# Attention values for two query blocks in one step, ten probability tiles, and another spread of the filling matmuls

## The chip, the cores and the metric

The kernel runs on one core of a Trainium2 chip. The metric is the device time of one execution in microseconds (us), the median of three runs. The core has five engines with instruction queues of their own: TensorE (PE in the profile, its weight loads PEld), VectorE (DVE), ScalarE (ACT), GpSimd (POOL) and SyncE (SP), which here issues the DMA transfers.

## The reference

`x` has 2048 tokens of 512 numbers. It is normalized; from the normalized `xn` comes an attention with 32 heads of 16 numbers over a sliding window of 256 keys, and a two-layer network whose output gates it:

```python
xn = layernorm(x)
q, k, v = split(xn @ wqkv)                      # 32 heads of 16
scores = q k^T / 4, kept where 0 <= i - j < 256
o = softmax(scores) @ v
s = o @ wo
g = silu(gelu(layernorm(xn) @ w1 + b1) @ w2 + b2)   # 512 -> 1792 -> 512
out = x + s * g
```

All inputs and outputs are 32-bit floats.

## The kernel before, in words

**Stages.** A short first stage normalizes `x`, transposes it (`xnT`) and makes the first queries, keys and values. Then comes the attention (72 to 448 us of the profiled execution), and after it the network and the gating.

**Slots.** The attention is one loop `for t in range(-16, end + 1)` whose passes are called slots here. The 32 heads are eight groups `n` of four heads; the 2048 tokens are sixteen blocks of 128. Slot `t` from 0 to 127 works on group `t // 16` and block `t % 16`. In program order a slot issues:

1. `prob_block(.., 1)`: two matmuls put the scores of one pair of heads (keys in the partitions, 384 queries) into `stb`, ScalarE takes their exponential into a tile `pt` (`ACT pt<-stb` in the profile), GpSimd clears the two corners outside the window (`affine_select`).
2. `max_block` for the block `LEAD` = 12 slots ahead: eight matmuls into `xy` and `zo`, then VectorE masks (`COPY_PREDICATED xy<-upper,zo`) and takes the maxima (`TENSOR_REDUCE mt<-xy`). Slots from 116 on have none.
3. `fill_in(t, 0)`: fills, matmuls of other work (`fb<-...`), and then the steps that are planned for this slot with `at`.
4. `prob_block(.., 0)`, the other pair of heads, into the same `stb`.
5. `fill_in(t, 1)`: more fills.
6. `pv_step` for block `t - 1`: values times probabilities of the three key blocks that the window touches, four heads side by side in column groups of 32 (17 weights columns each: 16 values and a column of ones for the sum). ScalarE copies the result out of PSUM (`oraw<-zo`).
7. Steps that are planned with `behind`, mostly DMAs.

Items 1 to 3 are called the first part of a slot here, items 4 to 7 the second part. `stb` exists once, so the scores of one part wait until ScalarE has read those of the part before. A matmul instruction of 32-bit floats (`pv_step`) is two passes in the profile, so the twelve of a step are recorded as x24; most other matmuls are of the type F32R and are recorded once.

**Dependencies by tile.** `otb`, in which `pv_step` accumulates, is a part of the PSUM tile `zo`; `max_block` uses another part of it. The built program makes the first matmul of `pv_step` wait for VectorE's masking of the same slot, and the next `max_block` matmul into `zo` wait for ScalarE's copy of `otb`.

**Fills.** `tandem(t0, t1, one, two)` lays two jobs over slots `t0` to `t1`: projections of queries and keys (`pair_qk`), of values (`pair_v`), or of the network's hidden layer (`pair_h`). Two matmuls with 64 rows each run side by side and make one unit; a tandem has two phases of 12 units (512 columns) or 24 (256 columns). Before, most units lie in the first part: typically three units of 512 columns there and one, two or three in the second part. At `t1` ScalarE and VectorE copy the two results out.

**Queries and keys.** `pair_qk(n, c).finish` plans, for a later slot `free`, a copy of the projection on ScalarE into a tile `sh` (`hi`, the rounded upper part), behind it four DMAs out of `sh` into the slot tile `qk` (`qk<-sh`), and in a slot given by `quiet` a subtraction on GpSimd that reads `sh` (`pjr<-pjr,sh`). `sh` has two buffers. The copies of jobs `c` and `c + 1` are two to four slots apart.

Of the kernel before, what the change touches and what calls it, by code (L numbers as in the profile page):

```python
# [9 lines left out]
F32 = mybir.dt.float32  # L10
F32R = mybir.dt.float32r
# [38 lines left out]
def mixer_kernel(ctx, tc, x, wqk, wv, wo, w1, b1, w2, b2, out):  # L50


    nc = SimpleNamespace(**{name: Ordered(tc, name) for name in ("tensor", "vector", "scalar", "gpsimd", "sync")})
# [6 lines left out]
    attn = ExitStack()  # L60
    psum = attn.enter_context(tc.tile_pool(name="psum", bufs=1, space=PSUM))
    vp = attn.enter_context(tc.tile_pool(name="vp", bufs=1))
    pp = attn.enter_context(tc.tile_pool(name="pp", bufs=8))
    sgp = attn.enter_context(tc.tile_pool(name="sgp", bufs=1))

    PASSES = ((0, 0), (0, 1), (1, 0))
# [78 lines left out]
    slots = []  # L145
# [16 lines left out]

    xy = psum.tile([P, 2, 512], F32, name="xy")
    zo = psum.tile([P, 2, 512], F32, name="zo")
    otb = zo[:, 1, 256:384]
    psf = attn.enter_context(tc.tile_pool(name="psf", bufs=1, space=PSUM))
    fb = [psf.tile([P, 512], F32, name=f"fb{i}") for i in range(2)]
    early = ExitStack()
# [99 lines left out]
    def job_qk(n, c):  # L268

        box = []  # L270
        ops = [(kt, a, b) for kt in range(KT) for a, b in PASSES]
        if not n and c < 2:
            ops.sort(key=lambda o: o[2])
        sl = slice(512 * c, 512 * (c + 1))

        def mm(i):
            if i == 0:
                box.append(fill_bank() if n or c else xy[:, 0])
            kt, a, b = ops[i]
            nc.tensor.matmul(box[0], wqs[n][:, a, kt], big[:, b, kt, sl],  # L280
                             start=(i == 0), stop=(i == len(ops) - 1))

        def send(src, qk, tt):
            copy_rows(slots[n % 2][tt:P:4, qk, :, sl], src[64 * qk: 64 * qk + 64])

        def finish():
            hi = sgp.tile([P, 512], F32R, tag="sh", name=f"sh_{n}_{c}", bufs=2)
            raw = t2.tile([P, 512], F32, tag="t2", name=f"pjr_{n}_{c}")
            lo = raw.bitcast(F32R)
            src = raw if n else box[0]  # L290
            if n:
# [38 lines left out]
    def pair_qk(n, c):  # L330

        ops = [(kt, a, b) for kt in range(KT) for a, b in PASSES]
        sl = slice(512 * c, 512 * (c + 1))

        def mm(ps, i, r, **flags):
            kt, a, b = ops[i]
            nc.tensor.matmul(ps, wqs[n][r, a, kt], big[r, b, kt, sl], **flags)

        def send(src, qk, tt):
            copy_rows(slots[n % 2][tt:P:4, qk, :, sl], src[64 * qk: 64 * qk + 64])  # L340

        def finish(ps, t, copy):
            hi = sgp.tile([P, 512], F32R, tag="sh", name=f"sh_{n}_{c}", bufs=2)
            raw = t2.tile([P, 512], F32, tag="t2", name=f"pjr_{n}_{c}")
            lo = raw.bitcast(F32R)
            copy(raw, ps)

            def send_high():
                if n >= 2:
                    copy_rows(slots[n % 2][3:P:32, 0, :, sl], slots[n % 2][7:P:32, 0, :, sl])  # L350
                for qk, tt in ((1, 0), (0, 0), (1, 2), (0, 1)):
                    send(hi, qk, tt)

            def send_low():
                send(lo, 1, 1)
# [45 lines left out]
                behind(t, nc.sync.dma_start, h_d[f - 6], raw)  # L401
        return 3 * KT, mm, finish

    def tandem(t0, t1, one, two, mid=None, back=None):

        n = one[0]
        lo, hi = slice(0, 64), slice(64, P)
        mid = mid or max(1, (t0 + t1 + 1) // 2)  # L410
        most = n // 4

        def places(slots, last):

            last = min(most, n // (len(slots) + 1)) if last else 0
            cuts = [(n - last) * k // len(slots) for k in range(len(slots) + 1)]
            out = []
            for t, a, b in zip(slots, cuts, cuts[1:]):
                ahead = min(b - a, max(most, (b - a + 1) // 2))
                out += [(t, 0)] * ahead + [(t, 1)] * (b - a - ahead)  # L420
            return out + [(t1, 0)] * last

        first, second = places(range(t0, mid), False), places(range(back or mid, t1), True)
# [63 lines left out]
    pts = {}  # L487
# [17 lines left out]
        pts[(n, kb, p)] = pt  # L505


    outs = {}
# [97 lines left out]
    def at(t, fn, *args):  # L606
        plan.setdefault(t, []).append((fn, args))
# [62 lines left out]
        fills.setdefault(place, []).extend(todo)  # L670
    soon = {}
    tandem(3, 8, pair_qk(1, 2), pair_qk(1, 3))
    for n, spans in enumerate((((9, 14), (15, 19)), ((20, 24), (25, 30)), ((31, 35), (36, 41)), ((42, 47), (48, 53, 51)),
                               ((75, 79), (80, 84)), ((85, 90), (93, 98))), 2):
# [4 lines left out]
    for f, *span in ((6, 99, 104, 102), (8, 105, 110), (10, 111, 115), (12, 116, 121, 118, 119), (2, 122, 127, 124, 125)):  # L679
# [544 lines left out]
```

## Time and profile before

| | before |
|---|---|
| median of 3 runs | 770.62 us (769.2 to 770.64) |
| profiled execution | 770.7 us |
| its span in the trace | 769.0 us |
| granted TensorE clock | 0.994 |
| busy: PE, PEld | 746.9 us (97%), 584.1 us (76%) |
| busy: DVE, ACT, POOL | 533.5 us (69%), 435.2 us (57%), 280.4 us (36%) |
| matmuls of `pv_step` (`zo<-pt,vt`) | 2880 records, 103.8 us busy |

Busy times of PE are unions of overlapping records whose ends are modelled; a busy PE need not be at its peak. The profile's lines `[0.33 <-ACT pt L42]` say how long the engine sat idle before an instruction and what released it. All instructions have line 42, that of a helper, so groups are told apart by their tiles.

### The profile page before, as it was taken

How to read it: one execution, taken by the hardware profiler on the slowest of the kernel's cores; microseconds unless marked ns; L12 is line 12 of the kernel's file. 1: busy time of each engine (PE TensorE's matmuls, PEld its weight loads, DVE VectorE, ACT ScalarE, POOL GpSimd, SP SyncE). 2: the span in 40 equal slices, each digit the busy share in tenths (PEclk: the TensorE clock that was granted, in tenths of full speed). 3: DMA queues.
4: the chain of work that ended last, by engine and by line, in shares of the span. 5: the costliest groups of instructions: out<-in, count | busy, mean ns of one | idle time of the engine just before them, and what ended most of it. 6: DMA issues, size and time to landing. Idle time of an engine off the chain costs nothing.

```text
span 769.0 us, 18778 instructions
## 1 busy us (share of the span) xinstructions
PE 746.9 (97%) x7428; PEld 584.1 (76%) x7428; DVE 533.5 (69%) x865; ACT 435.2 (57%) x724; POOL 280.4 (36%) x567
## 2 busy tenths in 40 slices
PE   9889999999999999999999999999999999999997
PEld 8777666666768887676676678888887888888886
DVE  7886777777777677887875447764657675576473
ACT  6536776767676675777876855444545553342001
POOL 6111666757656554665776800030101100001102
PEclk9989999999999999999999999999999999999999
DMA  7612444645446873454654274641202322243531
GB/s 260 206 44 51 108 106 124 175 114 141 99 103 180 271 225 100 103 156 125 168 156 148 62 267 140 182 160 42 83 20 78 122 73 93 83 155 123 174 96 55
DMA packets 56951, 99.40 MB, mean 129 GB/s; under 512 B 11104, under 2 KB 11360, under 8 KB 56864
## 3 DMA queue, kind: packets, MB, share of 16 engines
q1 hardware_dynamic: 56864, 98.21, 43.9%
q8 instruction: 58, 0.95, 0.5%
q14 instruction: 29, 0.24, 0.1%
HBM read 51.39 MB, written 29.62 MB: 105 GB/s over the span
## 4 chain that ended last, share of the span: by engine, by line
PE 84%; DVE 7%; ACT 4%; issue 2%; POOL 2%; DMA 1%; SPq 0%; DVEq 0%; ACTq 0%
PE acc L42 19%; PE fb L42 17%; PE zo L42 13%; PE p L42 9%; PE stb L42 8%; PE h L42 6%; PE s L42 6%; PE xy L42 5%; ACT pt L42 3%; DVE xy L42 1%; DVE mt L42 1%; PE pv L42 1%; DVE xnT L42 1%; POOL pt L42 1%; DVE bnA L42 1%
## 5 line engine op out<-in xcount | busy, mean ns | idle before, releaser
L42 POOL TENSOR_SCALAR_AFFINE_SELECT pt<-pt 128x256 f32<-128x256 f32 x480 | 193.0, 427 | 159.1 <-ACT pt L42 155.8
L42 ACT ACTIVATE pt<-stb 128x768 f32<-128x768 f32 (+1 forms) x244 | 188.7, 773 | 55.3 <-PE stb L42 46.2
L42 DVE TENSOR_REDUCE mt<-xy 128x4 f32<-128x1024 f32 (+1 forms) x128 | 152.6, 1192 | 4.4
L42 PE MATMUL acc<-w,gh 128*128 128x512 f32 x432 | 133.3, 390 | 0.0
L42 DVE COPY_PREDICATED xy<-upper,zo 128x512 f32<-128x512 int32 x112 | 77.5, 692 | 69.2 <-PE zo L42 67.3
L42 PE MATMUL fb<-xnT,wqb 64*128 64x512 f32 (+1 forms) x684 | 115.2, 405 | 0.5 <-DVE xnT L42 0.5
L42 PE MATMUL zo<-pt,vt 128*17 128x128 f32 x2880 | 103.8, 275 | 2.2 <-DVE xy L42 1.5
L42 PE MATMUL stb<-qk 64*128 64x384 f32 (+1 forms) x488 | 96.6, 392 | 7.1 <-ACT pt L42 5.7
L42 POOL TENSOR_TENSOR xo<-xo,gated 128x512 f32<-128x512 f32 x15 | 20.2, 1347 | 217.8 <-DVE gated L42 194.2
L42 PEld LDWEIGHTS zo<-pt,vt 128*17 128x17 f32 x2880 | 67.4, 97 | 39.4 <-issue 17.8
L42 PEld LDWEIGHTS acc<-w,gh 128*128 128x128 f32 x432 | 80.8, 188 | 16.5
L42 PEld LDWEIGHTS stb<-qk 64*128 64x128 f32 x488 | 45.5, 183 | 52.4 <-ACT pt L42 41.3
L42 PE MATMUL acc<-w,gl 128*128 128x512 f32 x216 | 84.2, 390 | 0.0
L42 PEld LDWEIGHTS fb<-xnT,wqb 64*128 64x128 f32 (+1 forms) x684 | 63.4, 186 | 7.4 <-DVE xnT L42 0.6
L42 PE MATMUL xy<-qk 64*128 64x256 f32 (+2 forms) x536 | 62.0, 305 | 4.9 <-DVE mt L42 4.4
L42 ACT COPY oraw<-zo 128x128 f32<-128x128 f32 x128 | 34.2, 267 | 40.4 <-PE zo L42 36.3
L42 PEld LDWEIGHTS xy<-qk 64*128 64x128 f32 x536 | 44.0, 186 | 16.7 <-DVE mt L42 9.6
L42 PEld LDWEIGHTS acc<-w,gl 128*128 128x128 f32 x216 | 40.5, 188 | 8.8 <-DVE gl L42 0.3
L42 ACT ACTIVATE gated<-acc 128x512 f32<-128x512 f32 x16 | 8.7, 596 | 65.1 <-DVE acc L42 65.1
L42 PE MATMUL s<-wos,ohl 128*128 128x512 f32 (+1 forms) x204 | 44.7, 377 | 0.0
L42 PEld LDWEIGHTS s<-wos,ohl 128*128 128x128 f32 x204 | 36.7, 188 | 7.0
L42 PE MATMUL zo<-qk 64*128 64x128 f32 x448 | 40.7, 259 | 0.0
(182 smaller groups left out, 1159.9 us busy)
## 6 DMA issues: line engine op xcount, KB each, us to landing
qk<-sh SPq DMA_DIRECT2D x128, 128.0 KB
qk<-pjr SPq DMA_DIRECT2D x64, 128.0 KB
oT_d<-oraw SPq DMA_DIRECT2D x32, 256.0 KB
w_d<-in_w_dram SPq DMA_DIRECT2D x14, 512.0 KB
x<-in_x_dram SPq DMA_DIRECT2D x16, 256.0 KB
or<-oT_d SPq DMA_DIRECT2D x16, 256.0 KB
w<-rden_d SPq DMA_DIRECT2D x16, 256.0 KB
xo<-in_x_dram SPq DMA_DIRECT2D x16, 256.0 KB
```

Of the source, the lines that this page charges most:

```text
L42: r = issue(*args, **kwargs)
```

## The change

`pv_step` is called at the end of every second slot (even `t` from 2) for two query blocks `t - 2` and `t - 1`. It works through four key blocks; two of them serve both query blocks with one matmul of 256 columns, two serve one with 128. `otb` is 256 columns wide, one copy takes it out, and every pair has its own output DMA. The probability tiles go from 8 to 10 buffers; `sh` goes from two buffers to one. `tandem` chooses the place of each unit by a running load of each part of a slot: 1.27 for the second part of an even slot, 0.5 for a first part with `max_block`, 0.25 more at `t1`, and 0.235 or 0.125 for each unit. A new function `seen` copies one column of each of the two fill banks at the start of the slot in which a tandem's second phase begins. Four tandems lose arguments that set where their phases lie.

```diff
-    pp = attn.enter_context(tc.tile_pool(name="pp", bufs=8))
+    pp = attn.enter_context(tc.tile_pool(name="pp", bufs=10))
...
-    otb = zo[:, 1, 256:384]
+    otb = zo[:, 1, 256:512]
...
-            hi = sgp.tile([P, 512], F32R, tag="sh", name=f"sh_{n}_{c}", bufs=2)
+            hi = sgp.tile([P, 512], F32R, tag="sh", name=f"sh_{n}_{c}", bufs=1)
...
-    def tandem(t0, t1, one, two, mid=None, back=None):
+    turns = set()
+
+    def seen(t):
+
+        for k in range(2):
+            nc.scalar.copy(small.tile([P, 1], F32, tag="seen", name=f"seen_{t}_{k}"), fb[k][:, 0:1])
+
+    def tandem(t0, t1, one, two, mid=None):
...
-        def places(slots, last):
-
-            last = min(most, n // (len(slots) + 1)) if last else 0
-            cuts = [(n - last) * k // len(slots) for k in range(len(slots) + 1)]
-            out = []
-            for t, a, b in zip(slots, cuts, cuts[1:]):
-                ahead = min(b - a, max(most, (b - a + 1) // 2))
-                out += [(t, 0)] * ahead + [(t, 1)] * (b - a - ahead)
-            return out + [(t1, 0)] * last
-
-        first, second = places(range(t0, mid), False), places(range(back or mid, t1), True)
+        def places(halves):
+
+            load = {}
+            for t, part in halves:
+                load[t, part] = (1.27 * (t % 2 == 0) if part else 0.5 * (t + LEAD < 16 * NQ)) + 0.25 * (t == t1)
+            count = dict.fromkeys(halves, 0)
+            for _ in range(n):
+                at_ = min(halves, key=lambda h: load[h])
+                load[at_] += 0.235 if n == 3 * KT else 0.125
+                count[at_] += 1
+            return [h for h in halves for _ in range(count[h])]
+
+        first = places([(t, part) for t in range(t0, mid) for part in range(2)])
+        second = places([(t, part) for t in range(mid, t1) for part in range(2)] + [(t1, 0)])
+        turns.add(mid)
...
     def pv_step(n, qb):
 
-        lo = max(qb - 2, 0)
-        for kb in range(lo, qb + 1):
+
+        for kb in (qb - 1, qb - 2, qb, qb + 1) if qb else (qb, qb + 1):
+            first, last = max(qb, kb), min(qb + 1, kb + 2)
             for j in range(4):
-                nc.tensor.matmul(otb[32 * j: 32 * j + DH + 1], vt[:, kb, (4 * n + j) % 16],
-                                 pts[n, kb, j // 2][:, j % 2, P * (qb - kb): P * (qb - kb + 1)],
-                                 start=(kb == lo), stop=(kb == qb),
+                nc.tensor.matmul(otb[32 * j: 32 * j + DH + 1, P * (first - qb): P * (last + 1 - qb)],
+                                 vt[:, kb, (4 * n + j) % 16],
+                                 pts[n, kb, j // 2][:, j % 2, P * (first - kb): P * (last + 1 - kb)],
+                                 start=(kb == max(qb - 1, 0)), stop=(kb >= qb),
                                  skip_group_check=True, tile_position=(0, 32 * j))
-        if qb % 4 == 0:
-            outs[0] = sgp.tile([P, 512], F32, tag="or", name=f"oraw_{n}_{qb}", bufs=2)
-        nc.scalar.copy(outs[0][:, P * (qb % 4): P * (qb % 4 + 1)], otb)
-        if qb % 4 == 3:
-            (at if n or qb > 7 else behind)(16 * n + qb + 2, nc.sync.dma_start, oT_d[n // 2, n % 2::2, :, P * (qb - 3): P * (qb + 1)], outs[0])
+        o = sgp.tile([P, 256], F32, tag="or", name=f"oraw_{n}_{qb}", bufs=2)
+        nc.scalar.copy(o, otb)
+        (at if n or qb > 6 else behind)(16 * n + qb + 3, nc.sync.dma_start,
+                                        oT_d[n // 2, n % 2::2, :, P * qb: P * (qb + 2)], o)
...
+        if t in turns:
+            seen(t)
         if 0 <= t < end:
...
-        if t >= 1:
-            pv_step((t - 1) // 16, (t - 1) % 16)
+        if t >= 2 and t % 2 == 0:
+            pv_step((t - 2) // 16, (t - 2) % 16)
```

More of the change, by code (lines that the diff above doesn't have):

```diff
@@ L342, in finish @@
         def finish(ps, t, copy):
-            hi = sgp.tile([P, 512], F32R, tag="sh", name=f"sh_{n}_{c}", bufs=2)
+            hi = sgp.tile([P, 512], F32R, tag="sh", name=f"sh_{n}_{c}", bufs=1)
             raw = t2.tile([P, 512], F32, tag="t2", name=f"pjr_{n}_{c}")
@@ L410, in tandem @@
         mid = mid or max(1, (t0 + t1 + 1) // 2)
-        most = n // 4
-        def places(slots, last):
-            last = min(most, n // (len(slots) + 1)) if last else 0
-            cuts = [(n - last) * k // len(slots) for k in range(len(slots) + 1)]
-            out = []
-            for t, a, b in zip(slots, cuts, cuts[1:]):
-                ahead = min(b - a, max(most, (b - a + 1) // 2))
-                out += [(t, 0)] * ahead + [(t, 1)] * (b - a - ahead)
-            return out + [(t1, 0)] * last
-        first, second = places(range(t0, mid), False), places(range(back or mid, t1), True)
+        def places(halves):
[11 more added lines that the diff above has]
+        turns.add(mid)
         for phase, where in enumerate((first, second)):
@@ L505, in prob_block @@
         pts[(n, kb, p)] = pt
-    outs = {}
     def pv_step(n, qb):
-        lo = max(qb - 2, 0)
-        for kb in range(lo, qb + 1):
+        for kb in (qb - 1, qb - 2, qb, qb + 1) if qb else (qb, qb + 1):
+            first, last = max(qb, kb), min(qb + 1, kb + 2)
             for j in range(4):
-                nc.tensor.matmul(otb[32 * j: 32 * j + DH + 1], vt[:, kb, (4 * n + j) % 16],
-                                 pts[n, kb, j // 2][:, j % 2, P * (qb - kb): P * (qb - kb + 1)],
-                                 start=(kb == lo), stop=(kb == qb),
+                nc.tensor.matmul(otb[32 * j: 32 * j + DH + 1, P * (first - qb): P * (last + 1 - qb)],
+                                 vt[:, kb, (4 * n + j) % 16],
+                                 pts[n, kb, j // 2][:, j % 2, P * (first - kb): P * (last + 1 - kb)],
+                                 start=(kb == max(qb - 1, 0)), stop=(kb >= qb),
                                  skip_group_check=True, tile_position=(0, 32 * j))
-        if qb % 4 == 0:
-            outs[0] = sgp.tile([P, 512], F32, tag="or", name=f"oraw_{n}_{qb}", bufs=2)
-        nc.scalar.copy(outs[0][:, P * (qb % 4): P * (qb % 4 + 1)], otb)
-        if qb % 4 == 3:
-            (at if n or qb > 7 else behind)(16 * n + qb + 2, nc.sync.dma_start, oT_d[n // 2, n % 2::2, :, P * (qb - 3): P * (qb + 1)], outs[0])
+        o = sgp.tile([P, 256], F32, tag="or", name=f"oraw_{n}_{qb}", bufs=2)
+        nc.scalar.copy(o, otb)
+        (at if n or qb > 6 else behind)(16 * n + qb + 3, nc.sync.dma_start,
+                                        oT_d[n // 2, n % 2::2, :, P * qb: P * (qb + 2)], o)
     mlp = {}
@@ L672, in mixer_kernel @@
     tandem(3, 8, pair_qk(1, 2), pair_qk(1, 3))
-    for n, spans in enumerate((((9, 14), (15, 19)), ((20, 24), (25, 30)), ((31, 35), (36, 41)), ((42, 47), (48, 53, 51)),
+    for n, spans in enumerate((((9, 14), (15, 19)), ((20, 24), (25, 30)), ((31, 35), (36, 41)), ((42, 47), (48, 53)),
                                ((75, 79), (80, 84)), ((85, 90), (93, 98))), 2):
@@ L678, in mixer_kernel @@
         tandem(t0, t1, pair_v(2 * i), pair_v(2 * i + 1))
-    for f, *span in ((6, 99, 104, 102), (8, 105, 110), (10, 111, 115), (12, 116, 121, 118, 119), (2, 122, 127, 124, 125)):
+    for f, *span in ((6, 99, 104, 102), (8, 105, 110), (10, 111, 115), (12, 116, 121), (2, 122, 127)):
         tandem(*span[:2], pair_h(f), pair_h(f + 1), *span[2:])
```

## The prediction

> **What bounds the kernel now.** I read the page first (span, busy times, chain), then the waits, then the timeline of single slots.
>
> ```profile
> span 769.0 us, 18778 instructions
> ...
> PE 746.9 (97%) x7428; PEld 584.1 (76%) x7428; DVE 533.5 (69%) x865; ACT 435.2 (57%) x724; POOL 280.4 (36%) x567
> ...
> PE 84%; DVE 7%; ACT 4%; issue 2%; POOL 2%; DMA 1%; SPq 0%; DVEq 0%; ACTq 0%
> ```
>
> By these lines TensorE is the bound, and any of its time that goes is gained. The waits say something else of the attention:
>
> ```profile
> ACT pt L42 <- PE stb L42: 46.2, 121, 1.0
> PEld stb L42 <- ACT pt L42: 41.3, 143, 1.3
> ```
>
> The scores wait for ScalarE 143 times and ScalarE for the scores 121 times: a loop, since `stb` exists once. The timeline of slots 16 to 18 shows its length, and nearly every price that I need:
>
> ```profile
> 122.21 0.44 PE L42 MATMUL stb<-qk 64*128 64x384 f32 x2
> ...
> 122.75 0.81 ACT L42 ACTIVATE pt<-stb 128x768 f32<-128x768 f32 x1
> ...
> 122.94 0.91 PE L42 MATMUL fb<-xnT,wqb 64*128 64x512 f32 x6
> 123.20 0.69 DVE L42 COPY_PREDICATED xy<-upper,zo 128x512 f32<-128x512 int32 x1 [1.28 <-PE zo L42]
> 123.46 0.61 ACT L42 CAST sh<-pjr 128x512 fp32r<-128x512 f32 x1
> 123.62 0.19 PEld L42 LDWEIGHTS stb<-qk 64*128 64x128 f32 x2 [0.20 <-ACT pt L42]
> 123.63 0.77 POOL L42 TENSOR_SCALAR_AFFINE_SELECT pt<-pt 128x256 f32<-128x256 f32 x2 [1.14 <-ACT pt L42]
> 123.69 0.38 PE L42 MATMUL stb<-qk 64*128 64x384 f32 x2
> ...
> 123.90 0.40 PE L42 MATMUL fb<-xnT,wqb 64*128 64x512 f32 x2
> 123.93 1.23 DVE L42 TENSOR_REDUCE mt<-xy 128x4 f32<-128x1024 f32 x1
> 124.11 0.81 ACT L42 ACTIVATE pt<-stb 128x768 f32<-128x768 f32 x1
> ...
> 124.23 0.41 PE L42 MATMUL zo<-pt,vt 128*17 128x128 f32 x8
> 124.36 1.27 POOL L42 TENSOR_TENSOR pjr<-pjr,sh 128x512 fp32r<-128x512 f32 x1
> ...
> 124.97 0.18 PEld L42 LDWEIGHTS stb<-qk 64*128 64x128 f32 x2 [0.61 <-ACT pt L42]
> 124.97 0.44 PE L42 MATMUL stb<-qk 64*128 64x384 f32 x2 [0.33 <-ACT pt L42]
> ...
> 125.51 0.81 ACT L42 ACTIVATE pt<-stb 128x768 f32<-128x768 f32 x1 [0.44 <-PE stb L42]
> ...
> 126.38 0.19 PEld L42 LDWEIGHTS stb<-qk 64*128 64x128 f32 x2 [0.18 <-ACT pt L42]
> ...
> 126.66 0.63 PE L42 MATMUL fb<-xnT,wqb 64*128 64x512 f32 x4
> ...
> 127.22 0.63 PE L42 MATMUL zo<-pt,vt 128*17 128x128 f32 x16
> ...
> 127.78 0.45 PE L42 MATMUL stb<-qk 64*128 64x384 f32 x2
> ```
>
> Slot 17 has a short values step (x8), so TensorE ran dry: the scores at 124.97 stood idle for 0.33 us until the exponential of 124.11 had ended at 124.92. This is the floor of a part: from the weight load at 123.62 to the one at 124.97 are 1.35 us (second part), from 124.97 to 126.38 are 1.41 (first part); a slot takes at least 2.76 us, whatever TensorE has to do. A full slot is hardly longer:
>
> ```profile
> 103.09 0.40 PE L42 MATMUL fb<-xnT,wqb 64*128 64x512 f32 x2
> ...
> 103.30 0.81 ACT L42 ACTIVATE pt<-stb 128x768 f32<-128x768 f32 x1 [0.54 <-PE stb L42]
> ...
> 103.42 0.85 PE L42 MATMUL zo<-pt,vt 128*17 128x128 f32 x24
> ...
> 104.20 0.19 PEld L42 LDWEIGHTS stb<-qk 64*128 64x128 f32 x2 [0.21 <-ACT pt L42]
> ```
>
> Here the exponential ends at 104.11 and the scores come at 104.20, as they do by TensorE's own work. The slots are packed so that the two bounds coincide at about 2.80 us. Slots 3 to 114 start and end at
>
> ```profile
> 81.24 0.81 ACT L42 ACTIVATE pt<-stb 128x768 f32<-128x768 f32 x1
> 414.47 0.81 ACT L42 ACTIVATE pt<-stb 128x768 f32<-128x768 f32 x1
> ```
>
> 333.2 us for 112 slots, 2.975 each: 0.2 us above the floor on average. That is all that less work on TensorE could bring here, about 22 us.
>
> **Part by part: the values.** x8, x16 and x24 take 0.41, 0.63 and 0.85 us: one pass of four heads at 128 columns is 0.11. Into the step: 0.33 from the last fill to it (123.90 to 124.23), where fill follows fill in 0.23 (x4 0.63 less x2 0.40), so 0.10 lost. Out of it: 0.78 from 103.42 to the scores at 104.20, six passes being 0.66, so 0.12; the first scores then take 0.45 in place of 0.38. Together 0.28 to 0.29 us a step, and 64 steps go: 18 us of TensorE.
>
> No matmul of 256 columns with two passes is in the trace. Its pass lies between 0.11 (the width is free) and 0.22 (twice 128). I take 0.22, by these rows:
>
> ```profile
> L42 PE MATMUL fb<-xnT,wqb 64*128 64x512 f32 x624 | 97.9, 404 | 0.5 <-DVE xnT L42 0.5
> L42 PE MATMUL fb<-wva,xnT 64*128 64x256 f32 x384 | 30.0, 283 | 0.0
> ```
>
> 97.9 / 624 is 0.157 a record at 512 columns, 30.0 / 384 is 0.078 at 256: time goes with columns. So a pair keeps its 12 passes' worth of columns, 1.31 us, now all in the second part of the even slot. That part becomes: scores 0.30, then 1.31, then 0.11 out, 1.72 us without one fill, against a floor of 1.35. TensorE exceeds the floor there by 0.37, and the first part, which ScalarE holds at 1.41, can't be shortened for it. The step's wait for VectorE's masking adds a little: the masking of slot 17 ended at 123.89, 1.68 after the scores of 122.21; the new step is ready 1.41 + 0.30 = 1.71 after them, so with the semaphore 0.04 late, and behind it queue the next scores. An even slot takes 1.41 + 1.72 + 0.04 = 3.17.
>
> Counted in the order of the two programs (960 matmul instructions of values where 1440 were, so the change is there), slots 3 to 114 have 49 even slots with a full step: 155.3 us, 0.9 more in six with many fills; seven with a half step at 2.80: 19.6. The 56 odd slots have the fills: the first part is 0.73 to the fills (122.21 to 122.94), 0.05 + 0.23 a unit, and 0.10 because the score matmuls into `zo` wait for a copy of 256 columns in place of 128:
>
> ```profile
> L42 ACT COPY oraw<-zo 128x128 f32<-128x128 f32 x128 | 34.2, 267 | 40.4 <-PE zo L42 36.3 <-DVE mt L42 2.9 <-DMA w_d<-in_w_dram 0.3
> L42 ACT COPY pjr<-fb 128x512 f32<-128x512 f32 x15 | 8.8, 586 | 5.8 <-PE fb L42 4.1 <-PE stb L42 1.7
> ```
>
> (586 - 267) / 384 is 0.83 ns a column, so 0.37 us in place of 0.27. The second part is 0.21 (123.69 to 123.90) + 0.05 + 0.23 a unit. 24 slots stay at 2.80, three at 2.82, 16 with three and five units take 1.57 + 1.41 = 2.98, five with three and six 3.21, eight others, mostly with value projections, sum to 24.7: 164.1 in all. Even and odd: 339.9. The same working for before (1.48 and 1.33 for three units and one, 0.23 for each more) gives 325.4 where 333.2 were measured; the 7.8 are copies and splits that lengthen single slots. I keep half, since the even slots now have slack on ScalarE and VectorE: 339.9 + 3.9 - 333.2 = **+10.6 us**. Bounds: 0 to 7.8 of the extras, and -18 (49 x 0.37) if the width were free.
>
> **One buffer for `sh`.** Now the copy of job c + 1 waits for the four DMAs and the subtraction of job c. In slot 17 the plan has both: the copy began at 123.46, the subtraction that reads the other buffer ended at 125.63. With one buffer the copy starts 2.2 us later, and behind it in ScalarE's queue stands the second exponential, for which the next scores wait. Slots 33 and 101 have the same pair. Slot 17 becomes 1.35 (first exponential done) + 0.09 + 0.77 + 1.28 on GpSimd + 0.65 copy + 0.81 + 0.06 = 5.0 against 2.98: 3 x 2.1 = 6.3. At slots 22 and 27 the DMAs are late instead:
>
> ```profile
> 150.69 2.49 SPq L42 DMA_DIRECT2D qk<-sh  x4
> 153.24 0.61 ACT L42 CAST sh<-pjr 128x512 fp32r<-128x512 f32 x1
> ...
> L42 SPq DMA_DIRECT2D out_dram<-xo x17: 332/339/449, 503.2 to 766.2; - x17
> ```
>
> The last issue ends at 153.18. Landing isn't shown; the last output issued at 766.2 has landed by 769.0, so it takes 0 to 2.8 us. At about 2 the copy is 1.9 late, less 0.34 for the longer even slot before: some 0.9 in slot 27 after its slack, 0.6 in slot 22. Sum **+8**, between 5 and 10. The Trainium skill, "TensorE: Matmul & The Clock Gate", section "Architectural detail", calls ACT and DVE strict FIFO. By that rule a waiting copy stops the exponentials behind it, which speaks against this change; slot 17 after will show it.
>
> **`seen`.** Two copies of one column, 0.16 us each by the 0.83 ns a column (267 - 128 x 0.83), at 20 slots before 115. After an even slot they queue behind the result's copy and push the exponential by 0.3 (eight times), otherwise by 0.1 (twelve times): **+3.5**, between 1 and 6.
>
> **The rest.** Slots 116 to 127 have no score maxima and two score buffers; TensorE bounds them, and six steps less give 6 x 0.28 = **-1.7**. Ten `pt` buffers: the tile that slot t writes was last read two steps of values earlier or in the slot just before, as now; nothing. Thirty-two more output DMAs on SyncE at 0.55 (four issues in 2.49 are 0.62 each) delay sends that are due slots later; nothing, up to 2. After 448 us nothing changes.
>
> Sum: 10.6 + 8 + 3.5 - 1.7 = 20.4, on the profiled execution's 770.7 (its span 769.0 and 1.7 around it), which is the median's 770.62 within 0.1: **791 us**.
>
> **Rivals.** (1) *TensorE is the bound after all*: the parts even out, the floor never binds and copies stall nothing; 770.7 - 18 = 753, or about 762 where half of the stalls remain. For it: 97% and 84%. Against: the idle 0.33 us of 124.97, and that even slots pay 0.37 each as soon as the second part is over 1.35. Chance 0.10. The Trainium skill, "TensorEngine Tiling (Array Packing)", section "Key Properties", says that changing the tiling mode drains TensorE; by that rule alone the gain is the same 64 drains, and the 0.28 here agrees. (2) *The width is free*: 49 x 0.37 = 18 less, 773. It decides if a 256-column pass takes under 0.15. Chance 0.06. (3) *One-buffer stalls are hidden*: 783, chance 0.14. (4) *Masking late*: VectorE's work left from the odd slot pushes the masking, and the values behind it, by 0.2 in 49 even slots: 801, chance 0.12. (5) The terms cancel: 770.7, 0.03. My forecast has 0.55.
>
> **Numbers.** What a measurement of this kernel tells from no change is about 0.2%, 1.5 us. Faster 0.11 (rival 1 and little else), same 0.04, slower 0.85. The range 773 to 803 leaves out rival 1 and a little above.
>
> **What would show it.** Right: `zo<-pt,vt` records with 256 columns near twice the pace; even slots near 3.17 and odd ones near 2.8 to 3.0; a wait of ACT `sh` on POOL `pjr` of about 2 us three times; more idle of PE before `stb`, released by ACT. Wrong: even slots at 2.8, `sh` copies without a wait, or TensorE without gaps in the attention.

## The result, and the profile after

| | time, median (lowest to highest) | ratio to before |
|---|---|---|
| before | 769.91 us (768.73 to 770.83) | |
| after | 806.76 us (804.49 to 807.77) | 1.0476 [1.0456, 1.0496] |

The change makes the kernel 4.8% slower. The forecast of 791 (773 to 803) had the direction, but was 16 us short, and the result lies 4 us above its range. The profiled execution of after took 807.45 us, its span is 805.7.

From the page of after come its span, its busy times, the clock that TensorE was granted, and the chain by engine:

```profile
span 805.7 us, 16862 instructions
...
PE 761.1 (94%) x6468; PEld 579.1 (72%) x6468; DVE 533.0 (66%) x865; ACT 429.4 (53%) x704; POOL 280.7 (35%) x567
...
PEclk9999998998999999999999999999999999999999
...
PE 75%; DVE 10%; ACT 6%; issue 3%; POOL 3%; DMA 2%; SPq 1%; DVEq 0%; ACTq 0%; POOLq 0%
```

TensorE has 960 records fewer and is busy for longer: 761.1 us against 746.9. Busy time is the union of the records, so fewer of them can fill more of it only if they last longer or overlap less; two causes below make the same matmuls slower. Its share of the chain falls from 84% to 75%, VectorE's rises from 7% to 10%. The waits of after say where VectorE came in:

```profile
ACT pt L42 <- PE stb L42: 71.1, 119, 1.8
PEld stb L42 <- ACT pt L42: 45.9, 107, 2.2
ACT sh L42 <- POOL pjr L42: 6.3, 3, 2.1
PE zo L42 <- DVE xy L42: 5.9, 13, 0.7
```

The loop between scores and exponentials is still there. New are the three waits of the copy into `sh`, 2.1 us each. The matmuls into `zo` wait for the masking 13 times and 5.9 us, where the same line of before has 5 times and 1.5 us. The weight loads ahead of them waited for the masking in before as well (`PEld zo L42 <- DVE xy L42`, 51 times, 16.6 us), so the wait as such isn't new; what it costs now is e7's question.

The windows view by stretch (length, busy time of each engine, granted clock, share of DMA, GB/s) gives slots 3 to 114, first of before, then of after:

```profile
81.20:414.50 333.30, 323.71 (x4976) 237.78 (x4976) 259.73 (x358) 237.40 (x409) 209.10 (x455) 1.00 0.53 143
```

```profile
81.30:445.20 363.90, 335.02 (x4139) 234.20 (x4138) 259.31 (x358) 231.88 (x393) 209.04 (x454) 0.96 0.49 131
```

The same slots take 30.6 us more, with 837 TensorE records fewer, and the mean clock in them is 0.96 in place of 1.00. After the last exponential a further 5.3 us are lost (329.9 us to the end, 324.6 before), at a full clock. The experiments take these apart.

### The profile page after: what moved, and what is told of

Its sections match the earlier page's. It is cut to its first block, busy times and chain, and to the rows that moved or that the text cites. A ratio compares the mean times of both kernels' runs of the same rounds, so it can differ in the third digit from the quotient of the medians.

```text
span 805.7 us, 16862 instructions
## 1 busy us (share of the span) xinstructions
PE 761.1 (94%) x6468; PEld 579.1 (72%) x6468; DVE 533.0 (66%) x865; ACT 429.4 (53%) x704; POOL 280.7 (35%) x567
## 4 chain that ended last, share of the span: by engine, by line
PE 75%; DVE 10%; ACT 6%; issue 3%; POOL 3%; DMA 2%; SPq 1%; DVEq 0%; ACTq 0%; POOLq 0%
PE acc L42 19%; PE zo L42 13%; PE fb L42 13%; PE p L42 8%; PE stb L42 6%; PE h L42 6%; PE s L42 5%; PE xy L42 3%; ACT pt L42 3%; DVE xy L42 3%; DVE mt L42 2%; POOL pt L42 1%; PE pv L42 1%; DVE xnT L42 1%; SPq L42 1%
## 5 line engine op out<-in xcount | busy, mean ns | idle before, releaser
L42 POOL TENSOR_SCALAR_AFFINE_SELECT pt<-pt 128x256 f32<-128x256 f32 x480 | 192.9, 427 | 190.5 <-ACT pt L42 181.6
L42 ACT ACTIVATE pt<-stb 128x768 f32<-128x768 f32 (+1 forms) x244 | 188.7, 773 | 75.0 <-PE stb L42 71.1
L42 DVE TENSOR_REDUCE mt<-xy 128x4 f32<-128x1024 f32 (+1 forms) x128 | 152.6, 1193 | 4.4
L42 DVE COPY_PREDICATED xy<-upper,zo 128x512 f32<-128x512 int32 x112 | 77.5, 692 | 95.9 <-PE zo L42 92.6
L42 PE MATMUL acc<-w,gh 128*128 128x512 f32 x432 | 136.5, 397 | 0.0
L42 PE MATMUL stb<-qk 64*128 64x384 f32 (+1 forms) x488 | 97.3, 393 | 19.6 <-ACT pt L42 14.3
L42 PE MATMUL fb<-xnT,wqb 64*128 64x512 f32 (+1 forms) x684 | 113.6, 415 | 0.3 <-DVE pjr L42 0.2
L42 PE MATMUL zo<-pt,vt 128*17 128x128 f32 (+1 forms) x1920 | 96.2, 341 | 7.6 <-DVE xy L42 5.9
L42 POOL TENSOR_TENSOR xo<-xo,gated 128x512 f32<-128x512 f32 x15 | 20.2, 1347 | 221.9 <-DVE gated L42 220.6
L42 PEld LDWEIGHTS acc<-w,gh 128*128 128x128 f32 x432 | 81.0, 188 | 19.2
L42 PEld LDWEIGHTS stb<-qk 64*128 64x128 f32 x488 | 47.2, 189 | 66.0 <-ACT pt L42 45.9
L42 PEld LDWEIGHTS zo<-pt,vt 128*17 128x17 f32 x1920 | 53.5, 100 | 50.7 <-issue 15.7
L42 PE MATMUL acc<-w,gl 128*128 128x512 f32 x216 | 85.6, 396 | 0.0
L42 PEld LDWEIGHTS fb<-xnT,wqb 64*128 64x128 f32 (+1 forms) x684 | 66.3, 190 | 8.9 <-DVE pjr L42 0.6
L42 PE MATMUL xy<-qk 64*128 64x256 f32 (+2 forms) x536 | 62.2, 306 | 7.9 <-DVE mt L42 7.1
L42 PEld LDWEIGHTS xy<-qk 64*128 64x128 f32 x536 | 45.8, 188 | 20.3 <-DVE mt L42 13.7
L42 ACT COPY oraw<-zo 128x256 f32<-128x256 f32 x64 | 23.9, 373 | 54.4 <-PE zo L42 48.2
L42 PEld LDWEIGHTS acc<-w,gl 128*128 128x128 f32 x216 | 40.7, 188 | 9.9
L42 PE MATMUL s<-wos,ohl 128*128 128x512 f32 (+1 forms) x204 | 44.8, 378 | 0.0
L42 ACT ACTIVATE gated<-acc 128x512 f32<-128x512 f32 x16 | 8.7, 596 | 66.1 <-DVE acc L42 66.1
L42 PE MATMUL zo<-qk 64*128 64x128 f32 x448 | 43.0, 269 | 0.2 <-ACT oraw L42 0.2
L42 PEld LDWEIGHTS s<-wos,ohl 128*128 128x128 f32 x204 | 36.7, 188 | 7.1
```

What stands on the lines that cost most here:

```text
L42: r = issue(*args, **kwargs)
```

## The experiments

Slot lengths are from the start of one slot's first exponential to the next slot's. (An even slot of after counts some 0.1 us long by this, and the odd slot behind it as much short: the copy of the values' result stands in ScalarE's queue ahead of the exponential that ends the even slot. Sums over both are not affected.) "Half" counts the stretches of half clock that begin in slots 3 to 114, each 3.41 us long (one of e7 6.83), in the execution that was profiled. The last column runs from the start of the last exponential to the end. Ratios are to runs of the kernel before on the same chip.

| run | time (us) | ratio | slots 3 to 114 | half | after the last exponential |
|---|---|---|---|---|---|
| before | 769.91 | | 333.2 | 0 | 324.6 |
| after | 806.76 | 1.0476 [1.0456, 1.0496] | 363.9 | 8 | 329.9 |
| e0 before again | 771.25 (one run) | | 333.5 | 0 | 324.5 |
| e1 copies apart | 796.81 | 1.0347 [1.0326, 1.0369] | 353.4 | 5 | 330.0 |
| e2 before, one `sh` | 780.57 | 1.0120 [1.0081, 1.0160] | 344.3 | 2 | 324.8 |
| e3 values in halves | 790.26 | 1.0260 [1.0226, 1.0295] | 348.0 | 3 | 329.8 |
| e4 `seen` of 64 bytes | 804.10 | 1.0427 [1.0412, 1.0443] | 363.8 | 8 | 326.5 |
| e5 before, shifted | 776.03 | 1.0057 [1.0035, 1.0079] | 333.1 | 0 | 329.3 |
| e6 array kept busy | 803.48 | 1.0430 [1.0402, 1.0459] | 361.1 | 3 | 329.9 |
| e7 masking apart | 794.20 | 1.0298 [1.0275, 1.0322] | 351.8 | 5 | 329.9 |
| e8 four causes removed | 777.76 | 1.0097 [1.0075, 1.0119] | 334.5 | 0 | 329.2 |
| e9 before, fills by load | 771.53 | 1.0007 [0.9996, 1.0018] | 334.2 | 0 | 324.5 |
| e10 `seen` last | 801.20 | 1.0395 [1.0367, 1.0424] | 363.7 | 8 | 325.9 |
| e11 four removed, in place | 773.76 | 1.0035 [1.0022, 1.0048] | 334.3 | 0 | 325.7 |

**e0_before_again.** The kernel before, unchanged, profiled a second time.

> The kernel before, unchanged, profiled again. In its first profile full-width matmuls after the attention follow each other every 226.9 ns on average; in the profile of the changed kernel every 230.7 ns, at a granted clock of 1.00 in both, which makes 5 us of the difference. Theory 1 (a difference between runs or chips, not the kernel): this profile too can show 227 to 231 ns. Theory 2 (a consequence of the change): 226.9 ns again, and 769 to 771 us.

Slots 3 to 114 took 333.5 us, the last part 324.5, and no half clock fell in the slots. The two losses belong to the changed kernel.

**The one buffer of `sh`: e1_copies_apart and e2_before_one_buffer.** The first takes the stalls out of after, the second puts the buffer's loss alone into before.

```diff
 # e1, in after
+            free = max(free, held[0] + 3, held[1] + 1)
+            held[0] = free
             at(free, nc.scalar.copy, hi, raw)
             behind(free, send_high)
             free = quiet(max(free, t + 1))
+            held[1] = free
 # e2, in before (both places)
-            hi = sgp.tile([P, 512], F32R, tag="sh", ..., bufs=2)
+            hi = sgp.tile([P, 512], F32R, tag="sh", ..., bufs=1)
```

> The changed kernel, with the rounded copies into the one buffer of sh at least three slots apart and after the subtraction that reads the buffer, all else as it is. Theory 1 (the one buffer stalls ScalarE in slots 17, 27, 33 and 101, 7 us in all, and the idle TensorE then gets half the clock for 3.41 us in slots 18, 34 and 102, 3.4 us more): 795 to 799 us, no wait of the copies on GpSimd, fewer stretches at half clock. Rival (the stalls only shift idle time that the slots have anyway): 804 to 808 us.

> The kernel before with one buffer for sh in place of two, nothing else. Theory 1: the copies of slots 17, 22, 27, 33 and 101 wait 1.3 to 2.2 us each: 8 us of stalls and up to 4 us of half clock behind them, 777 to 783 us. Rival (hidden): 769 to 772 us.

The timeline of after shows slot 17, the prediction's example:

```profile
123.78 0.81 ACT L42 ACTIVATE pt<-stb 128x768 f32<-128x768 f32 x1
...
125.39 1.28 POOL L42 TENSOR_TENSOR pjr<-pjr,sh 128x512 fp32r<-128x512 f32 x1
126.70 0.62 ACT L42 CAST sh<-pjr 128x512 fp32r<-128x512 f32 x1 [2.11 <-POOL pjr L42]
127.22 0.80 ACT L42 ACTIVATE pt<-stb 128x768 f32<-128x768 f32 x1
128.08 0.19 PEld L42 LDWEIGHTS stb<-qk 64*128 64x128 f32 x2 [2.21 <-ACT pt L42]
128.08 0.45 PE L42 MATMUL stb<-qk 64*128 64x384 f32 x2 [1.78 <-ACT pt L42]
```

ScalarE stood idle for 2.11 us until GpSimd's subtraction ended at 126.67; the exponential of 127.22 queued behind its copy, and TensorE stood for 1.78 us behind the exponential. The slot took 4.79 us. The times of e1 and e2 (796.81 and 780.57) fell into their theories' ranges. In e1 the slot takes 2.77, and of the 10.5 us that e1's slots give back 7.6 lie in slots 17, 27, 33 and 101; another 2.8 lie in slots 18, 34 and 102, which ran at half clock behind those stalls. In e2 the same wait appears in a kernel with none of the other edits, and the slots lengthen by 11.1 us, of which 7.0 lie in slots 17, 27, 33 and 101 and 2.6 in slots 34 and 102 with their half clock:

```profile
125.92 0.62 ACT L42 CAST sh<-pjr 128x512 fp32r<-128x512 f32 x1 [2.10 <-POOL pjr L42]
```

**e3_values_spread: is TensorE the bound?** The pair's values are issued in two halves, one at the end of each slot, so that no part of a slot has more than 0.66 us of them. The second half's start clears what the first half had summed, so the older key blocks' part is left out of the sums; the number of matmuls is that of after.

```diff
+        kbs = ((qb - 1, qb - 2) if qb else ()) if half == 0 else (qb, qb + 1)
-        if t >= 2 and t % 2 == 0:
-            pv_step((t - 2) // 16, (t - 2) % 16)
+        if t >= 1:
+            q = t - 1 - (t + 1) % 2
+            pv_step(q // 16, q % 16, (t + 1) % 2)
-                load[t, part] = (1.27 * (t % 2 == 0) if part else ...
+                load[t, part] = (0.9 if part else ...
```

> The changed kernel, with the pair's values in two halves: the two older key blocks at the end of the odd slot, the two newer ones at the end of the even slot, six passes each; the running load of the fills counts 0.9 for every second part. The wide matmuls stay, the number of mode changes is that of before. Theory 1 (the even slot's second part of 1.95 us against a floor of 1.35 costs about 17 us, and sparse odd slots get half the clock): 780 to 788 us, slots near 2.8 without alternation; what is left over 770 is the one buffer. Rival (TensorE is the bound, so mode changes cost): 64 x 0.28 = 18 us more than the changed kernel, 820 to 826 us.

The time is 2 us over the expected 780 to 788, and the rival's 820 is out. Seven slots with or behind a stall of `sh` (17, 27, 28, 33, 34, 101, 102) hold 13.6 us over before. With those at before's lengths the slots sum to 334.4, where before has 333.2: neither the fewer matmul instructions nor their even spread made the slots shorter in sum.

**e6_array_kept_busy: the half clock.** Matmuls without a use are laid into seven odd slots that have next to no fills.

```diff
+        if t in (19, 35, 41, 47, 53, 63, 79):
+            for _ in range(6):
+                nc.tensor.matmul(zo[:, 0, 256:384], ident, ident, start=True, stop=True)
```

> The kernel after with six matmuls of the identity by itself (128x128, results not used) in the second part of the odd slots 19, 35, 41, 47, 53, 63 and 79, which hold next to no fills and no values step. Theory (the half clock of slots 20, 36, 42, 48 and 80 comes because TensorE idled in the sparse odd slot ahead of it): the stretches of half clock at 136.0, 190.6, 211.1, 231.6 and 330.6 us go, those behind the stalled slots (129.2, 183.8, 402.3) stay; slots 20, 36, 42, 48 and 80 fall from 4.9-5.6 to 3.3-3.7 us, slots 3 to 114 from 363.9 to 356-358, and the time from 806.8 to 799-801. Rival (the half clock is called up by the load of the even slots themselves, by the 32 wide matmuls behind one another, and work added before them makes it no rarer): as many stretches, 806-810.

First what the half clock is. The windows view of after, two stretches behind one another in slots 47 and 48:

```profile
228.15:231.56 3.41, 2.08 (x22) 1.47 (x22) 3.01 (x7) 2.19 (x5) 1.43 (x4) 1.00 0.13 38
231.56:234.97 3.41, 3.41 (x38) 1.52 (x36) 1.88 (x3) 0.81 (x1) 0.93 (x3) 0.51 0.23 52
```

In the first TensorE has 2.08 us of 3.41 to do; in the second it is busy throughout, at a clock of 0.51. The timeline of after gives the price in slot 48, beside the same step in slot 10:

```profile
103.43 1.49 PE L42 MATMUL zo<-pt,vt 128*17 128x256 f32 x32
...
229.59 0.44 PE L42 MATMUL stb<-qk 64*128 64x384 f32 x2 [0.90 <-ACT pt L42]
...
232.51 2.70 PE L42 MATMUL zo<-pt,vt 128*17 128x256 f32 x32
```

Slot 47 has two fill matmuls and no values. TensorE waits 0.90 us there for an exponential, and the values of slot 48 then take 2.70 us in place of 1.49; the slot takes 5.63. The timeline of e6 has the same step at

```profile
226.14 1.50 PE L42 MATMUL zo<-pt,vt 128*17 128x256 f32 x32
```

With slot 47 filled, slot 48 is back at 3.25 us. Slots 20, 36, 42, 48 and 80 fall by 10.2 us in all, all to 3.15 to 3.25. The half clock comes on a grid of 3.41 us (last section). Each stretch of e6's grid that ends in one of these slots or the slot ahead was busy for 84% or more, where those of after were busy for 61% to 70%, so the theory of their half clock holds. Its other half does not: of the three stretches that were to stay, those in slots 18 and 34 went as well (2.4 us), with no matmul added there, behind stretches that were busy for 60% and 62%. The expected time (799 to 801) was still missed by 2.5 us, for the twelve passes of 0.11 us lengthened the seven odd slots by 5.8, and slots 27, 28, 87 and 88 grew by 4.8, with two stretches of half clock at places where after has none.

**e7_mask_apart: the values' wait for VectorE.** The masking no longer reads the PSUM bank into which the values are summed.

```diff
-                                  neg if qb < 2 else zo[:, :, 0:256].rearrange(...))
+                                  neg)
```

> The kernel after, but the masking of the maxima copies the constant in place of the oldest key block's scores, so that the maxima leave that key block out, and VectorE no longer reads the PSUM bank into which the values are summed. Theory (the first values matmul of an even slot waits for the masking that reads scores of the same bank, 0.15 us in most of them and 0.4 to 0.7 in the sixteen where the masking is late): the median gap from the second part's first scores matmul to the first values matmul falls from 0.54 to 0.37-0.39, slots 24, 40, 72, 92, 96, 104 and 108 fall from about 4.0 to 3.4, slots 3 to 114 from 363.9 to 354-357, and the time from 806.8 to 797-800. Rival (the values wait for the probabilities of the second exponential anyway, and the masking ends in the same shadow): less than 3 us, 804-807.

Slot 24, in the timeline of after and then of e7:

```profile
150.01 0.44 PE L42 MATMUL stb<-qk 64*128 64x384 f32 x2
...
150.30 0.67 DVE L42 COPY_PREDICATED xy<-upper,zo 128x512 f32<-128x512 int32 x1
...
151.11 1.50 PE L42 MATMUL zo<-pt,vt 128*17 128x256 f32 x32 [0.66 <-DVE xy L42]
```

```profile
146.44 0.44 PE L42 MATMUL stb<-qk 64*128 64x384 f32 x2
...
146.81 1.50 PE L42 MATMUL zo<-pt,vt 128*17 128x256 f32 x32
```

In after the values start 1.10 us after the scores, when the masking (to 150.97) is over; in e7 after 0.37. The slot falls from 3.96 to 3.23 us. The median of that gap over 49 even slots, counted from the weight load of the scores, falls from 0.54 to 0.375 (slot 92 alone keeps 0.96). The waits view of after names GpSimd's `pt` for 31 waits of the weight loads into `zo`, 15.5 us in all, but in 37 of the 49 slots the values start 0.15 us after the masking's end, and in none of e7's. The gaps sum to 9 us less, counted from the scores' matmuls, slots 3 to 114 to 12.1 us less, and the time falls by 12.6, more than the theory's 7 to 10. Part of it is the clock, which falls on other slots here: 18, 42, 48, 80 and 102 run at full clock in e7 without a matmul added ahead of them, while 27, 28 and 54 grew. So the masking's price lies between 9 and 12 us. The edit takes away a wait of the masking too, which no longer needs the scores in `zo`; the two weren't separated.

**The part after the attention: e4_seen_padded, e5_before_shifted, e10_seen_last.** The new `seen` tiles take 96 bytes of a partition ahead of everything allocated later.

```diff
 # e4, in after (192 bytes in place of 96)
-            nc.scalar.copy(small.tile([P, 1], F32, tag="seen", ...), fb[k][:, 0:1])
+            nc.scalar.copy(small.tile([P, 16], F32, tag="seen", ...)[:, 0:1], fb[k][:, 0:1])
 # e5, in before (96 bytes in place of none)
+    for i in range(3):
+        nc.vector.memset(small.tile([P, 8], F32, tag="pad", ...), 0.0)
 # e10, in after (none ahead)
+            nc.scalar.copy(sgp.tile([P, 1], F32, tag="seen", ..., bufs=3), fb[k][:, 0:1])
```

> The kernel after with each `seen` tile made 64 bytes wide in place of 4 (three of them now take 192 bytes of a partition in place of 96), so that every tile that is allocated later in a partition (the values' weights vt, the probabilities, and all tiles of the part after the attention) starts at a multiple of 64 bytes again, as in the kernel before, and not 32 bytes past one; nothing that is computed changes. Theory A (the 5.3 us after the attention come from where the operands of TensorE's matmuls lie in a partition): the spacing of the 512-column matmuls after the attention returns from 230.7 to 226.9 ns, that part from 329.9 to about 324.6, and the time from 806.8 to 801-802; the values' matmuls may gain a little too. Rival B (it comes from something else that the change carries into the tail, such as the order of the transfers or a clock state left by the attention): 806-808, spacing 230.7.

> The kernel before with three unused tiles of 32 bytes (cleared once by VectorE at the start) in the pool of the small tiles, so that every tile allocated later lies 96 bytes further in its partition, 32 bytes past a multiple of 64, as in the kernel after. Theory A (place of the operands): the part after the attention 324.6 to about 330, spacing of its 512-column matmuls 226.9 to 230.7 ns, time 769.9 to 775-776. Rival B (something else): 769-771, spacing 226.9.

> The kernel after with the `seen` tiles taken from the last pool of the attention (sgp) in place of the pool of small tiles, so that the tiles of the part after the attention lie at the very addresses that they have in the kernel before (shift 0). So far the spacing of the matmuls of acc after the attention went with the shift of their weights gh and gl against the kernel before: 226.8 ns at 0 bytes, 234.1 at 96, 233.0 at 128, 229.6 at 192. Theory A (place alone): spacing 226.8 in acc, the part after the attention 324.6, slots 3 to 114 as in after (362-364), time 801-802. Rival B (the shift is not it, but something that the change carries there): 806-808.

The groups of the largest matmuls of that part (shortest, median and longest record in ns, first and last start), in before, after, e5 and e10:

```profile
L42 PE MATMUL acc<-w,gh x432: 387/389/476, 459.5 to 752.8; 128*128 128x512 f32 x144
```

```profile
L42 PE MATMUL acc<-w,gh x432: 392/397/478, 491.4 to 789.5; 128*128 128x512 f32 x144
```

```profile
L42 PE MATMUL acc<-w,gh x432: 392/397/478, 459.8 to 757.9; 128*128 128x512 f32 x144
```

```profile
L42 PE MATMUL acc<-w,gh x432: 387/389/476, 491.6 to 785.7; 128*128 128x512 f32 x144
```

A shift of 96 bytes makes their median record 8 ns longer, in a kernel before that has nothing else of the change; taken back in after, it is gone. From start to start these matmuls take 226.9 ns in before and 234.1 in after and e5; with the 216 of `acc<-w,gl` the means are 226.9 and 233.9, and 648 times 7.0 is 4.5 us. Theory A holds for the place. Its rule does not: with e4's 192 bytes, a multiple of 64, this group keeps 229.6 ns, and with e8's 128 bytes 233.0. In e10 the part is still 1.3 us longer than in before, with the old spacing; where that comes from stays open. Which distance between `gh`, `gl` and the operand `w`, which wasn't moved, is a good one stays open. The values' matmuls gained nothing: slots 3 to 114 are as long in e4 and e10 as in after.

**e9_before_even_fills.** The third part of the change alone, with a load that suits a step of values in every slot.

```diff
 # in before: places(halves) of the change, with
+                load[t, part] = (0.9 if part else 0.5 * (t + LEAD < 16 * NQ)) + 0.25 * (t == t1)
```

> The third part of the change alone, in the kernel before (one block's values each slot, two buffers of sh): the fills are laid by load, a second part counted at 0.9 us in every slot, a first part at 0.5, in place of the fixed portions. Theory (the slots are at their floor of 2.7-2.8 us where they hold up to eight fills, and each fill beyond costs 0.12, so a more even spread of the same fills takes little): slots 3 to 114 between 330 and 334, time 767-771. Rival 1 (the laying by load itself is a cost, as its first parts get fewer and its second parts more): 774-778. Rival 2 (it is a real gain that the other parts of the change hid): 760-765.

771.53 us is no difference that can be told from none (1.0007, 0.9996 to 1.0018). Laying the fills by load is neither the gain nor the loss.

**e8_four_removed and e11_four_removed_in_place.** All causes together: e1's and e7's edits, three matmuls in place of e6's six, and for the place an unused tile (e8) or e10's edit (e11).

> The kernel after with the four suspected causes taken away together: hi copies at least three slots apart, the maxima masked with the constant (they leave out the oldest key block), three matmuls of the identity in the second part of the seven sparse odd slots, and one unused tile of 32 bytes so that everything allocated later starts at a multiple of 128 bytes, as in the kernel before. Theory (these four are the whole loss): taking for each of the slots 3 to 113 the shortest that one of the earlier versions of after had, they sum to 327 us where the kernel before has 330; so slots 3 to 114 at 330-337, the part after the attention 324.6 with a spacing of 226.9 ns, and the time 768-776, the kernel before within 1%. Rival A (the causes cover the same stretches, and with one gone another takes its place, or the pair of blocks has a cost of its own of 5.9 us a pair over 5.6): slots 3 to 114 at 340-348, time 780-788. Rival B for the tail alone (64 bytes is what matters, and e4's 228.0 ns has another cause): spacing 228, part after the attention 326.5.

> As e8, but with the shift taken away by taking `seen` from the last pool, in place of the unused tile: copies apart, maxima masked with the constant (without the oldest key block), three matmuls of the identity in seven odd slots. Theory (the 4.6 us that e8 had after the attention were the place): part after the attention 324.6, spacing 226.8 in acc, slots 3 to 114 as in e8 (334-335), time 772-774. Rival (e8's rest has another cause): 776-779.

e8's slots (334.5) are as the theory had them; its time isn't (777.8 for 768 to 776). One reason is the part after the attention, 329.2 us for 324.6, since 128 bytes were hardly better than 96. The other lies in executions that have no profile: the profiled one took 775.1 at a mean clock of 0.998, the slowest 779.3 at 0.994. e11 came out at 773.76, and the windows view of its slots 3 to 114 is

```profile
81.90:416.20 334.30, 325.10 (x4182) 230.45 (x4182) 265.22 (x358) 231.69 (x394) 209.22 (x454) 1.00 0.53 144
```

334.3 us with 794 records fewer than before in 333.3: with every loss found taken away, the pair of blocks is still no faster; the kernel is 0.35% slower. Nothing tried beats the kernel before.

## Why the prediction was wrong, point by point

| term | forecast | measured | from |
|---|---|---|---|
| values, fills and `seen`, slots 3 to 114 | +10.6 and +3.5 | +10.0 | e1's 353.4 less 10.2 of half clock (e6), less 333.2 |
| one buffer of `sh` | +8 | +7.6 | e1, slots 17, 27, 33, 101 |
| half clock | none | +13.0 | 10.2 in slots 20, 36, 42, 48, 80 (e6), 2.8 in 18, 34, 102 (e1) |
| slots 115 to 127 | -1.7 | +0.6 | 30.6 to the last exponential, 30.0 before |
| after the attention, and before slot 3 | 0 | +5.4 | e5, e10; 0.1 of it before slot 3 |
| sum | 20.4 | 36.6 | 805.7 - 769.0 = 36.7 |

**The steps that failed.** Two terms that the sum put at nothing, the clock and the part after the attention, cost 13.0 and 5.4 us; they are more than the 16 us by which the forecast was short. Slots 115 to 127 add 2.3 to that, and the row of the values takes 4.1 off. The clock was left out without a reason; "After 448 us nothing changes" looked at what is computed there and not at where its tiles lie. Inside the row of the values a third step failed, the wait for the masking, and was hidden by others.

**What bounds the kernel: right.** The prediction set the loop of scores and exponentials against the page's 97%. The busy share can't decide it, for in e11 TensorE is busy as long as before (325.1 us for 323.7) with 794 records fewer. The slots do: counted from scores to scores, e11's odd slots sum to 4.7 us less than before's and those with a half step to 1.6 less, while its 49 full even slots sum to 7.3 more. The odd slots without many fills stop at a median of 2.76 us, the floor that the prediction read from slot 17. Of what the values free in the odd slots, ScalarE's loop lets only these 4.7 us through, and what they add in the even ones counts in full; e3, which spreads them evenly, ends at the same 334 us once the stalls are taken off. The "rival 1" (753 to 762) fell with it, and so did rival 2, for the pass of 256 columns is 0.22: in the timeline of after the 32 records of slot 10 take 1.49 us with the last one's tail, 1.22 from the first start to the last.

**Even and odd slots: right but for the masking, and the sum by luck.** The prediction's prices run from scores to scores, so the slots are counted that way here. Where nothing waits for the masking and the clock is full, the even slots came out as forecast: 154.6 us in e11 for the 49, where the forecast of 156.2 (155.3 and 0.9) has 154.2 without its 2.0 for the wait. In e1 they sum to 173.7, or 163.5 with the 10.2 of half clock taken off. The difference to e11, 8.9 us, is by this working the wait. The step that failed is "with the semaphore 0.04 late": it was worked out for the parts of slot 17, with VectorE free. In after VectorE often has earlier work in front of the masking, the wait adds 0.16 us to the median gap and 0.7 in slots like 24, and in all 9 to 12 us where 49 times 0.04 is 2. That is rival 4's mechanism at its size.

It didn't give rival 4's time, because the 56 odd slots gave as much back: they sum to 160.2 in e1, where 164.1 and 3.9 of extras were forecast. The extras didn't come, and slots 47, 63, 79 and 95 took 2.2 to 2.4 us for the 2.80, since the scores of a group's last block have 128 columns in place of 384. The other prices held: 15 slots with three units and five took 2.95 in the median for the 2.98, and their fills start 0.83 us after the scores in after and 0.73 to 0.77 in before, which is the 0.10 for the longer copy. That the row of the values came out 4.1 us under its forecast, and so close, is luck: extras that didn't come and a price for `seen` that doesn't show covered a wait that was priced too low.

The Trainium skill, "PSUM — Partial Sum Buffer", section "PSUM bank collisions raise a hardware error", says that the chip doesn't arbitrate two engines on one bank and that software has to keep them apart. The trace fits what follows from it, the values standing 0.66 us for a masking that only reads other columns of their bank; whether the chip needs that wait no run here shows.

**`sh`: right, in place and size.** Three waits of 2.1 us in the named slots, 1.2 in slot 27 for the 0.9 forecast, none to speak of in 22. Slot 17 took 4.79 for the 5.0.

**`seen`: too high.** The two copies take 0.23 us together in ScalarE's queue, where it has slack; no loss of theirs can be seen in the +10.0, though they weren't taken out alone. Their price was elsewhere: of the 5.3 us behind the attention 4.0 (e10) to 4.7 (e5) come from the 96 bytes that their tiles take.

**The clock: not in the sum at all.** The prediction counted every idle stretch of TensorE at its own length. Eight of them were followed by 3.41 us at half clock, which cost 1.6 us apiece. Its "after 448 us nothing changes" failed as well, on where tiles lie rather than on what is done.

**The fills' new places and ten `pt` buffers: nothing,** as assumed (e9 for the fills; the buffers weren't tried alone). That TensorE's time "of 18 us" brings nothing is the part of the forecast that carried the sign.

## What to carry to other kernels

Work taken from an engine that is 97% busy is worth nothing where a loop between two other steps has the same length; look for the floor in a slot where that engine runs dry. Work that is bunched costs three times over: in the crowded part, in the wait that its longer hold on a shared bank and buffer makes, and in the clock, if the emptied part leaves TensorE idle for a third of a few microseconds. And a tile of a few bytes, allocated early, moves all the others: compare the mean record of unchanged matmuls before and after. Last, count slots between the same two events as the forecast does, or a queue shared by both shifts time from one to the next.

## What the runs showed of the hardware that was not expected

**The half clock comes on a fixed grid and from partial idleness.** All 43 stretches of half clock that begin between 81 and 440 us in the fourteen profiles (eight of them have some) last 3.41 us or twice that, and their starts within a profile lie whole multiples of 3.413 us apart. In the 3.41 us ahead of each TensorE was busy for 29% to 70% of the time, by records whose ends are modelled; none began behind a busier stretch, though the long one of e7 went on behind 82%, busy at half clock. The share alone doesn't decide: full clock followed on stretches of 53% to 70% too. Nor do the slots: the grid lies elsewhere against them in each execution, so after has a half clock in slot 42 and none in 64, and e10, with slots as long, one in 64 and none in 42. The Trainium skill, "TensorE: Matmul & The Clock Gate", section "What's actually happening", has a window of 3413 ns that runs freely, and the grid agrees. Its section "HAM oscillation — how this bites in real kernels" puts the rule as no idle gap over about 3.4 us; here the longest gap ahead of slots 20, 36, 42, 48 and 80 of after was 0.9 us each time (229.59 above), so that rule is too mild for this kernel.

**Where a matmul's weights lie changes its pace.** Shifts of 0, 96, 128 and 192 bytes of `gh` and `gl` gave 226.9, 234.1, 233.0 and 229.6 ns from start to start for the same 512 columns (the first group, `acc<-w,gh`). The work was the same; the cause inside the memory wasn't found.
